# Sliding-window attention and a gated MLP: the first three units in parts of DFF, weight words decoded in place, queues ordered by another pass

## The chip, the cores and the metric

The kernel runs on one core of one Trainium2 chip. The metric is the device time of one execution in microseconds (us); a time that is given for a kernel is the median of several runs. The engines are named as in the profile: PE (TensorE) with its weight loads PEld, DVE (VectorE), ACT (ScalarE), POOL (GpSimd), and SP (SyncE), whose queue issues the transfers between DRAM and the on-chip memory.

## The reference

An attention in which each position sees itself and the 63 positions before it, then a gated MLP with a convolution over three positions:

```python
scores = scale * np.matmul(q, k.transpose(0, 1, 3, 2))   # B=8, H=8, S=576, D=64
mask = (rel >= 0) & (rel < 64)                            # rel = pos_q - pos_k
scores = np.where(mask, scores, -1000000000.0)
scores = scores - np.max(scores, axis=-1, keepdims=True)
attn = np.exp(scores)
attn = attn / (np.sum(attn, axis=-1, keepdims=True) + 1e-09)
x = np.matmul(attn, v)                                    # to [B, S, 512]
h = np.maximum(x @ w_in, 0.0)                             # w_in 512 x 1024
conv_out += conv_w[k] * hp[:, k:k + S, :]                 # k = 0, 1, 2; hp is h with a zero row at both ends of a sequence
gate = 1.0 / (1.0 + np.exp(-conv_out))
out = h * gate @ w_out                                    # w_out 1024 x 512
```

The activations are float32. The three weight tensors are float64, and they come to the chip as words of 64 bits, which the kernel decodes itself.

## The kernel before, in words

**Units.** The 8 x 576 positions are cut into 12 units of 384 (NX). A unit goes through attention, the first matmul with `w_in` (mm1), relu, convolution, sigmoid gate, the second matmul with `w_out` (mm2), and a store. DFF = 1024 is cut into 8 slices of 128 (f, NF), DM = 512 into 4 of 128 (c for mm1's sums, o for mm2's outputs, NC).

**Attention of a unit** has three blocks b of four window tiles. For each block: scores into two PSUM banks (`qk`, L357, called "sc" on PE); the row maximum with the mask on DVE (L364); eight exponentials with their row sums on ACT (L374); a guard on the sums (L377), the reciprocal (L380) and the normalising (L385). Then the weights of the attention are turned over. Units 0 and 1 (`BY_PE = 2`) are "wide": blocks of 128 x 128, turned by six groups of TensorE transposes a unit (L391), each copied out of PSUM by ACT (`untile`, L396). The other units have narrower blocks (96 of 128), which DVE transposes in 32 x 32 squares into `tbuf` (L412), and which 24 small DMAs a unit put into `ub` (`place`, L424). At last values (L488): for each c twelve small matmuls into a bank `acc`, which is split into a larger part `xh` (ACT, L492) and what is left, `xl` (DVE, L495).

**MLP of a unit.** Every large product is made of three: larger by larger, smaller by larger, larger by smaller. So mm1 has for each f 3 x 4 matmuls of 384 columns (L508) into one of the two banks `acc`; relu on ACT (L525, L529) writes `hbuf`; POOL carries the two edge columns from one unit to the next (L514 to L520). For each pair of slices ACT does the middle tap (L535), DVE the side taps (L542), ACT the sigmoid (L549, with a table load where the exponential stood before it) and DVE the gate (L554); ACT and DVE split the result into `gh` and `gl` (L558, L562). mm2 (L571) sums in four banks `po`, 3 matmuls for each f and o, five slices behind mm1 (`LAG`). At the end of a unit ACT and DVE copy the four banks to `ot` (L607, L609) and SP stores it.

**The decoding of weights** (`to_f32`, `weights`): the words of a pair of slices land in one of two staging buffers `bits`, ACT takes the absolute value of the upper half as float (L252), POOL the maximum with a tiny number (L253), DVE shifts (L254) and sets the sign (L256), ACT scales the lower half (L259), DVE adds it (L260). The larger part is cast by ACT (L275) or POOL (L277), the smaller subtracted by DVE (L278). `bits`, `tbuf` and `ot` share one tile, which the profile calls T.

**The order** of every engine's queue is fixed before the run. `queued` goes through all steps as a list scheduler with a cost for each: of the steps that could begin next on an engine it takes the one with the smallest due time `t`. The due times count in slices of mm1; for the first units and the attention they are the numbers of a table, `START`. `SWITCH` and `LEAVE` are its costs for going from one sort of matmul to another and for ACT's tables. At the beginning, where TensorE would wait, it puts in matmuls on a spare tile, whose results nobody reads (`keep_busy`, L216).

Of the kernel before, what the change touches and what calls it, by code (L numbers as in the profile page):

```python
# [28 lines left out]
LAG = 5  # L29
BY_PE = 2  # L30
# [3 lines left out]
TINY = 2.0 ** -15  # L34

LAST = NU - 1
# [10 lines left out]

class Work:


    def __init__(self, t, eng, cost, do, r, w, kind, mb, port):
        self.t, self.eng, self.cost, self.do, self.r, self.w, self.kind, self.mb = t, eng, cost, do, r, w, kind, mb
        self.port = port
        self.needs, self.after, self.ready = 0, [], 0.0
        self.start = self.end_ = 0.0


def queued(works, fill=None):

    import heapq
    writer, readers = {}, {}
    for x in works:
        deps = set()
        for k in x.r:
            if k in writer:  # L70
                deps.add(writer[k])
        for k in x.w:
            deps.update(readers.get(k, ()))
            if k in writer:
                deps.add(writer[k])
        deps.discard(x)
        for d in deps:
            d.after.append(x)
        x.needs = len(deps)
        for k in x.w:  # L80
            writer[k], readers[k] = x, []
        for k in x.r:
            readers.setdefault(k, []).append(x)
    free = {"PE": 0.0, "DVE": 0.0, "ACT": 2.0, "POOL": 0.7, "SP": 1.3}
    state = dict.fromkeys(free)
    waiting = {e: [] for e in free}
    touched = {k: ("", 0.0) for k in [("sc", 0)] + [("acc", i) for i in range(2)] + [("po", i) for i in range(NC)]}
    for x in works:
        if x.needs == 0:
            waiting[x.eng].append(x)  # L90
    dma, port, order, left = 0.0, {"DVE": 0.0, "POOL": 0.0}, [], len(works)
    while left:
        best = None
        for e, ws in waiting.items():
            if not ws:
                continue
            start = max(free[e], min(x.ready for x in ws))
            if best is None or start < best[0]:
                best = (start, e)
        start, e = best  # L100
        x = min((x for x in waiting[e] if x.ready <= start),
                key=lambda x: x.t - (0.5 if x.kind and x.kind == state[e] else 0.0))
        if x.port:
            if e == "POOL" and start < port["DVE"]:
                free[e] = port["DVE"]
                continue
            start = max(start, port["POOL"])
            port[e] = start + x.port
        waiting[e].remove(x)
        if fill and e == "PE" and start < FILL_TO:  # L110
            t = max(free[e], FILL_FROM)
            n = int((start - t) * FILL)

            clean = [(end, k) for k, (by, end) in touched.items() if by != "PE" and end < t]
            if n > 0 and clean:
                order.append(Work(x.t, e, 0.0, fill(n, min(clean)[1]), [], [], None, 0, 0.0))
        turn = SWITCH[e] if e in SWITCH and (x.kind != state[e] if e == "PE" else x.kind and x.kind != state[e]) else 0.0
        if turn and e == "PE" and not x.kind:
            turn = LEAVE
        if e == "PE" or x.kind:  # L120
            state[e] = x.kind
        end = free[e] = start + turn + x.cost * (1.75 if e == "PE" and start < WARM else 1.0)
        if x.mb:
            dma = max(dma, start) + x.mb * 2.7
            end = dma + 1.9
        for k in x.r + x.w:
            if k in touched:
                touched[k] = e, end
        order.append(x)
        left -= 1  # L130
        for y in x.after:
            y.needs -= 1
            y.ready = max(y.ready, end + (0.0 if e == "PE" else 0.06) if y.eng == e else end + 0.2)
            if y.needs == 0:
                waiting[y.eng].append(y)
    return order
# [3 lines left out]
START = {  # L140
    "v0": -34.213,
    "pv0": -15.486,
    "conv": -34.622,
    "bits": ((-44.162, -48.108), (-49.962, -46.523)),
    "qk1": -44.058,
    "v1": -6.318,
    "qk2": 0.918,
    "qk0": (-88.698, -55.197, -55.435),
    "ex0": (-38.484, -35.539, -25.91),
    "sc1": (-35.664, -14.916, -14.661),  # L150
    "ex1": (-10.948, -3.722, -2.234),
    "mask": -13.894,
    "sig": ((5.143, 6.743, 8.637, 10.624), (2.954, 4.077, 7.59, 9.996), (4.046, 6.806, 8.285, 10.314)),
    "in": (-40.063, -38.679, -33.327, -12.569, -5.818),
    "out": (-5.241, -4.847, 7.996, 9.148),
    "pv": ((4.028, 4.396, 3.657, 4.79), (6.11, 6.569, 6.573, 6.956), (3.166, 4.869, 3.456, 4.567)),
    "ex": ((6.203, 9.564, 10.485), (7.867, 9.835, 9.841), (5.299, 6.578, 7.215)),
    "qk": ((1.316, 5.641, 4.209), (5.897, 6.102, 6.617), (3.205, 3.444, 5.13)),
}
SWITCH = {"PE": 0.14, "ACT": 1.28}  # L160
LEAVE = 0.24
PORT_CL = 0.5
WARM = 5.0
FILL, FILL_FROM, FILL_TO = 4.0, 2.0, 110.0
FILL_COLS = 512, 384, 256
# [3 lines left out]
def attention_moe(ctx: ExitStack, tc: tile.TileContext, q, k, v, w_in, conv_w, w_out, out):  # L169
    nc = tc.nc  # L170

# [7 lines left out]
    xh, xl = many(2, [P, NC, NX], F32R, "xh"), many(2, [P, NC, NX], F32R, "xl")  # L179
    hbuf = pool.tile([P, NF, NG + 2], F32, name="hbuf")  # L180
    wih, wil = pool.tile([P, NF, NC, P], F32R, name="wih"), pool.tile([P, NF, NC, P], F32R, name="wil")
    woh, wol = pool.tile([P, NF, DM], F32R, name="woh"), pool.tile([P, NF, DM], F32R, name="wol")
    cw = pool.tile([P, 3, NF], F32, name="cw")
    mask = many(3, [P, P], F32, "mask")
    ident = pool.tile([P, P], F32, name="ident")
    qs = pool.tile([P, NC, NX], F32, name="q")
    ks = pool.tile([P, NC, NX + W], F32, name="k")
# [4 lines left out]
    ghs, gls = many(3, [P, 2, NG], F32R, "gh"), many(3, [P, 2, NG], F32R, "gl")  # L192


    flat = pool.tile([P, 16 * NT * 32 + NC * NG], F32, name="T")
    tbuf = flat[:, :16 * NT * 32].rearrange("p (g j t q) -> p g j t q", g=2, j=4, q=32)
    ot = flat[:, 16 * NT * 32:].rearrange("p (o n) -> p o n", o=NC)
    bits = [flat.bitcast(U32)[:, 4 * DM * i:4 * DM * (i + 1)].rearrange("p (e two) -> p e two", two=2) for i in range(2)]
    T_BITS = (0,), (0, 1)
    w24 = many(2, [P, 2 * DM], F32, "w24")  # L200
    cbits = pool.tile([P, 3 * NF, 2], U32, name="cbits")
    sc = many(2, [P, 512], F32, "sc", psum)
    acc = many(2, [P, 512], F32, "acc", psum)
    po = many(NC, [P, 512], F32, "po", psum)

    spare = pool.tile([P, 512], F32R, name="spare")
    filled = [0]
# [94 lines left out]

    def wide(u):
# [429 lines left out]
```

## Time and profile before

| | |
|---|---|
| time, median of 3 runs | 528.75 us (527.37 to 530.91) |
| the profiled execution, span from its first to its last instruction | 528.6 us |
| TensorE clock granted, mean over the span | 0.994 |
| moved by the DMA queues | 69.94 MB, mean 132 GB/s |
| HBM read and written | 47.73 MB and 9.47 MB |

The profiled execution's own time is its span, 528.6 us; what lies around the span isn't in the profile, and the span is 0.15 us from the median of the runs. The rows in the prediction come from the page of this execution and from questions to its trace. A row of a group (an operation with its line, its count, then busy time and mean ns of one, then the idle time of its engine ahead of it) speaks of the whole span; a row in order of time begins with its start in us and its duration. Line numbers are those of the code above.

### The profile page before, as it was taken

To read this page: it belongs to the slowest core of one execution; us is meant where nothing else is said; L and a number is where in the kernel's file an instruction comes from. 1 tells how busy PE (TensorE), PEld (TensorE's weight loads), DVE (VectorE), ACT (ScalarE), POOL (GpSimd) and SP (SyncE) were. 2 spreads that over 40 slices of the span, in tenths; PEclk is the share of its full clock that TensorE was granted. 3 is DMA by queue.
4 is the path that set the end of the run, shared out by engine and by line. 5 is a ranking of instruction groups with operands and counts; after the bars stand their busy time and mean duration, and the time that the engine had idled before them with its cause. 6 is when DMAs were issued, how large, how long until landed. Compare 5 with 4: busy or idle time off the path is not lost.

```text
span 528.6 us, 14478 instructions
## 1 busy us (share of the span) xinstructions
PE 507.8 (96%) x5646; PEld 486.1 (92%) x5646; DVE 377.7 (71%) x1084; ACT 384.5 (73%) x1017; POOL 105.5 (20%) x192
## 2 busy tenths in 40 slices
PE   6867899999999999999999999999999999999996
PEld 4657799999899999999999999999999999999996
DVE  3998999998668676667767767767767767655552
ACT  1988999788795994696696697687687687544541
POOL 5663645112011120011021021021021021000000
PEclk9998999999999999999999999999999999999999
DMA  8982670265472264172173073083073053010011
GB/s 275 378 276 101 231 258 2 51 203 190 115 269 68 66 206 129 56 275 69 40 288 77 22 256 112 23 287 97 14 279 99 24 165 95 13 61 1 1 61 60
DMA packets 29459, 69.94 MB, mean 132 GB/s; under 512 B 5712, under 2 KB 17616, under 8 KB 29392
## 3 DMA queue, kind: packets, MB, share of 16 engines
q1 hardware_dynamic: 29392, 69.03, 39.6%
q8 instruction: 44, 0.72, 0.6%
q14 instruction: 23, 0.19, 0.1%
HBM read 47.73 MB, written 9.47 MB: 108 GB/s over the span
## 4 chain that ended last, share of the span: by engine, by line
PE 89%; DMA 4%; ACT 3%; DVE 2%; issue 1%; SPq 0%; ACTq 0%
PE po L571 39%; PE acc L508 38%; PE acc L488 6%; PE sc L357 5%; DMA q<-in_q_dram 2%; DMA T<-in_w_in_dram 1%; DVE s L364 1%; ACT ub L396 1%; ACT s L374 0%; ACT w L252 0%; DVE wil L278 0%; DVE w L260 0%; DVE xl L495 0%; DVE s L385 0%; ACT L374 0%
## 5 line engine op out<-in xcount | busy, mean ns | idle before, releaser
L508 PE MATMUL acc<-xh,wih 128*128 128x384 f32 x384 | 132.2, 344 | 1.8 <-ACT hbuf L529 0.9
L542 DVE SCALAR_TENSOR_TENSOR c<-hbuf,cw,c 128x386 f32<-128x386 f32 (+1 forms) x192 | 110.0, 624 | 32.8 <-ACT c L535 32.7
L571 PE MATMUL po<-gh,woh 128*128 128x386 f32 (+1 forms) x384 | 132.3, 345 | 0.0
L508 PE MATMUL acc<-xh,wil 128*128 128x384 f32 x384 | 130.9, 341 | 0.0
L508 PE MATMUL acc<-xl,wih 128*128 128x384 f32 x384 | 130.6, 340 | 0.0
L571 PE MATMUL po<-gh,wol 128*128 128x386 f32 (+1 forms) x384 | 129.8, 338 | 0.0
L571 PE MATMUL po<-gl,woh 128*128 128x386 f32 (+1 forms) x384 | 129.8, 338 | 0.0
L374 ACT ACTIVATE s<-s,nm 128x96 f32<-128x96 f32 (+2 forms) x288 | 105.4, 370 | 5.1 <-DVE nm L364 4.9
L508 PEld LDWEIGHTS acc<-xh,wih 128*128 128x128 f32 x384 | 72.9, 190 | 3.5 <-issue 2.1
L562 DVE TENSOR_TENSOR gl<-c,gh 128x772 fp32r<-128x772 f32 (+1 forms) x48 | 54.9, 1144 | 28.6 <-ACT gh L558 28.3
L571 PEld LDWEIGHTS po<-gh,woh 128*128 128x128 f32 x384 | 72.2, 188 | 2.9
L508 PEld LDWEIGHTS acc<-xl,wih 128*128 128x128 f32 x384 | 73.0, 190 | 0.0
L508 PEld LDWEIGHTS acc<-xh,wil 128*128 128x128 f32 x384 | 72.9, 190 | 0.0
L385 POOL TENSOR_TENSOR s<-s,r 128x768 f32<-128x768 f32 x27 | 39.7, 1471 | 165.4 <-DVE r L380 154.1
L554 DVE TENSOR_TENSOR c<-c,hbuf 128x772 f32<-128x772 f32 (+1 forms) x48 | 47.0, 980 | 36.0 <-ACT c L549 35.9
L571 PEld LDWEIGHTS po<-gl,woh 128*128 128x128 f32 x384 | 72.3, 188 | 0.0
L571 PEld LDWEIGHTS po<-gh,wol 128*128 128x128 f32 x384 | 72.3, 188 | 0.0
L529 ACT ACTIVATE hbuf<-acc 128x384 f32<-128x384 f32 x64 | 30.8, 484 | 46.2 <-PE acc L508 45.9
L549 ACT ACTIVATE c<-c 128x772 f32<-128x772 f32 (+1 forms) x48 | 40.7, 848 | 27.4 <-DVE c L542 27.2
L364 DVE CUSTOM_DVE_ANT_0 s<-sc,mask 128x96 f32<-128x96 f32 (+2 forms) x272 | 51.6, 254 | 9.0 <-POOL mask L328 5.3
L374 ACT ACTIVATION_READ_ACCUMULATOR s<-s,nm 128x1 f32 x288 | 55.2, 192 | 0.0
L535 ACT ACTIVATE c<-hbuf,cw 128x386 f32<-128x386 f32 (+1 forms) x96 | 53.6, 609 | 0.0
(64 smaller groups left out, 576.2 us busy)
## 6 DMA issues: line engine op xcount, KB each, us to landing
v<-in_v_dram SPq DMA_DIRECT2D x24, 768.0 KB, 7.1
ub<-T SPq DMA_DIRECT2D x240, 48.0 KB, 2.0
k<-in_k_dram SPq DMA_DIRECT2D x22, 448.0 KB, 5.6
q<-in_q_dram SPq DMA_DIRECT2D x22, 384.0 KB, 5.8
out_dram<-T SPq DMA_DIRECT2D x8, 772.0 KB, 4.4
T<-in_w_in_dram SPq DMA_DIRECT2D x8, 512.0 KB, 6.9
T<-in_w_out_dram SPq DMA_DIRECT2D x8, 512.0 KB, 5.1
out_dram<-T SPq DMA_DIRECT2D x3, 768.0 KB, 6.2
```

The source lines that it names most:

```text
L364: nc.vector.tensor_tensor_reduce(out=ss[b][:, i, h, o:n], in0=banks_of(u, b)[h][:, i * P + o:i * P + n], in1=mask[m][:, o:n], scale=-0.125 ...
L374: nc.scalar.activation(x, x, AF.Exp, bias=nms[b][:, e], scale=-1.0, accum_out=sms[b][:, e])
L385: on.tensor_tensor(sv, sv, rs[b].unsqueeze(2).broadcast_to([P, 2 * NB, n]), ALU.mult)
L488: nc.tensor.matmul(acc[bank(("v", u, c))][h * D:(h + 1) * D, t * W:(t + 1) * W], vs[:, c, t, h], ub[g][:, 2 * p:2 * p + 2, 2 * t + h], sta ...
L508: nc.tensor.matmul(acc[bank(("m", u, f))][:, :NX], w[:, f, c], x[u % 2][:, c], start=(c == 0 and j == 0), stop=(c == NC - 1 and j == 2))
L529: nc.scalar.activation(hbuf[:, f, o:o + NX], ps[:, :NX], AF.Relu)
L535: nc.scalar.activation(cs[i % 2][:, a, :n], hbuf[:, f, 1:1 + n], AF.Copy, scale=cw[:, 1, f:f + 1])
L542: nc.vector.scalar_tensor_tensor(c, hbuf[:, f, e:e + n], cw[:, e, f:f + 1], c, op0=ALU.mult, op1=ALU.add)
L549: nc.scalar.activation(c, c, AF.Sigmoid)
L554: nc.vector.tensor_tensor(c, c, hbuf[:, 2 * i:2 * i + 2, 1:1 + n], ALU.mult)
L562: nc.vector.tensor_tensor(gls[ring(u, i)][:, :, :n], cs[i % 2][:, :, :n], ghs[ring(u, i)][:, :, :n].bitcast(F32), ALU.subtract)
L571: nc.tensor.matmul(po[o][:, :n], w[:, f, es], x, start=(f == 0 and j == 0), stop=(f == NF - 1 and j == 2))
```

## The change

**The first three units in parts.** `TASKS` replaces "for each unit all eight slices". Units 0, 1 and 2 go over slices 0 and 1 in turn, then over 2 and 3, then over 4 to 7; units 3 to 11 are as before. mm2 sums in PSUM only within a part. The result of a first part is stored plainly by SP (`store`), those of the second and third parts are added to it in DRAM by six transfers that POOL issues (`store_more`). `xh` and `xl` exist three times. All result copies go half to ACT and half to DVE, through one tile `ot`, which now stands by itself.

**Weights.** The words of a slice f are loaded into a tile of their own, `raw_in f` or `raw_out f`, in whose place the larger and the smaller part are put later (`w_in f`, `w_out f`, the same tag). The two buffers in between (`wx`) share tile T with `tbuf` only. POOL's maximum goes; a factor 2^-112 in ACT's absolute value does its work. The list `HI` says which engine casts the larger part of each of nine groups, `DECODE` the groups.

**Attention.** Units 0 to 2 are wide (`BY_PE = 3`) and their queries and keys come block by block from a new input, `first`, packed on the host. Unit 0 is normalised in halves, unit 3 on DVE too (`POOL_FROM = 4`). A `place` DMA is a step of its own.

**Order.** `plan` writes the steps without due times, `link` finds what each waits for, `backward` goes from the end to the beginning and gives each step the latest time at which it may start, `OFF` corrects that for some fifty steps, and `schedule` is the list scheduler with these as priorities, with costs of its own, with a bonus (`STICK`) for a step of the same sort as the last one on PE or ACT, and with a choice of PSUM banks. `START` is left for scores, transposes (`turn`) and values.

```diff
-LAG = 5
-BY_PE = 2
 NB = 4
 NBU = 2 * NT // NB
 MASKED = -8.0e9
-TINY = 2.0 ** -15
...
+BY_PE = 3
+SPLIT = 3
+CUTS = [(0, 2), (2, 4), (4, NF)]
+LAG = 5
+TASKS = [(u, a, b) for a, b in CUTS for u in range(SPLIT)] + [(u, 0, NF) for u in range(SPLIT, NU)]
...
+    def decode(key, fs):
+        n, one = len(fs), len(fs) == 1
+        kx = ("x", turn[0] % 2)
+        buf = turn[0] % 2
+        turn[0] += 1
...
+            load("load_w", (key, f), 0.524, [(key, f), (key, f, "lw")])
+        args = (key, fs, buf)
+        at("ACT", 0.03 + 0.5 * n, 0.14 + 0.5 * n, "magnitude", args, r=raw, w=[kx])
...
+        eng = HI[len(decoded_in)]
...
+    for k, (u, f0, f1) in enumerate(TASKS):
+        if u not in done:
+            done.add(u)
+            attention(u)
...
+        n = width_of(u)
+        x = x_of(u)
+        po = [Group([(4 + o,)]) for o in range(NC)]
+        for f in range(f0, f1):
+            need("in", f)
...
+                for ff in fs:
+                    need("out", ff)
+                    for o in range(NC):
+                        at("PE", 0.527, 0.7, "mm2", (u, ff, o, j, ff == f0, ff == f1 - 1), r=[("gh", g), ("gl", g), ("out", ff, "h"), ("out", ff, "l")] + [("pob", o)],
+                           w=[("po", k, o)], grp=po[o], t=first[k] + ff - f0 + LAG + 0.5 + 0.01 * o)
...
+        part = "more" if f0 else "first"
...
+            at(e, 0.365 if e == "ACT" else 0.477, 0.48 if e == "ACT" else 0.56, "result", (u, o, e), r=[("po", k, o)], w=[("ot", o), ("pob", o)], grp=po[o])
...
+        if part == "more":
+            at("POOL", 1.2, 1.2, "store_more", (u,), r=[("ot", o) for o in range(NC)], w=[("out", u)], mb=1.2)
+        elif u != LAST:
+            load("store", (u,), 0.8, [("out", u)], r=[("ot", o) for o in range(NC)])
...
+def schedule(works, prio, fill=False):
...
+                p = prio[x]
+                if x.kind and x.kind == kind.get(e):
+                    p -= STICK
+                if best is None or s < best[0] - 1e-9:
+                    best = (s, p, x)
+                elif s <= best[0] + 1e-9 and p < best[1]:
+                    best = (best[0], p, x)
...
+def backward(works):
...
+HI = ('POOL', 'POOL', 'POOL', 'POOL', 'ACT', 'ACT', 'ACT', 'DVE', 'POOL')
+DECODE = [('in', (0,)), ('in', (1,)), ('out', (0, 1)), ('in', (2, 3)), ('out', (2, 3)), ('in', (4, 5)),
+          ('out', (4, 5)), ('in', (6, 7)), ('out', (6, 7))]
+HALVED = (0,)
+POOL_FROM = 4
+GUARD_TO = 3
+WARM = 16.0
+FILL, FILL_FROM, FILL_TO = 0.45, 2.0, 110.0
...
+    flat = pool.tile([P, 2 * 3 * 2 * NT * 32], F32, name="T")
+    wx = [flat[:, 2 * DM * i:2 * DM * (i + 1)] for i in range(2)]
+    tbuf = flat.rearrange("p (g j t q) -> p g j t q", g=2, j=3, q=32)
...
+        raws[key, f] = pool.tile([P, DM, 2], U32, name=f"raw_{key}{f}", tag=f"{key}{f}")
...
+    def load_first(u, b):
+        a, n, _ = first_at(b)
+        nc.sync.dma_start(qk[:, a:a + n], first[u, :, a:a + n])
...
+    def to_magnitude(x, hw):
+        nc.scalar.activation(x, hw.bitcast(F32), AF.Abs, scale=2.0 ** -112)
...
+    def to_shift(x):
+        xu = x.bitcast(U32)
+        nc.vector.tensor_scalar(xu, xu, 3, 0x7FFFFFF8, op0=ALU.logical_shift_left, op1=ALU.bitwise_and)
...
+    def larger(kf):
+        wts[kf] = pool.tile([P, 2, DM], F32R, name="w_%s%d" % kf, tag="%s%d" % kf)
+        return wts[kf][:, 0]
...
-        at(t, "POOL", 0.0027 * n + 0.02, lambda: nc.gpsimd.tensor_scalar(x, x, TINY, None, op0=ALU.max), w=kt, port=PORT_CL)
...
-            xu, xu, 3, 0x3FFFFFF8, op0=ALU.logical_shift_left, op1=ALU.bitwise_and), w=kt)
...
+    def store_more(u):
         n = width_of(u)
+        nc.gpsimd.dma_start(out[u, :, :, :n], ot[:, :, :n], accum_op=ALU.add)
...
+    works = plan()
+    late = backward(works)
+    for x in works:
+        late[x] += OFF.get((x.fn,) + x.args[:2], 0.0)
     with tc.manual_schedule():
-        for x in queued(plan, keep_busy):
-            x.do()
+        for x in schedule(works, late, True)[0]:
+            fn[x.fn](*x.args, *([x.grp.banks] if x.grp else []))
```

Three places of the new queues. The first is ACT's queue ahead of the first pairs of gate halves. In both kernels `s`, `sm` are exponentials, `ub` copies of transposes, `hbuf` relu, `c` the middle tap or the sigmoid, `xh` value halves and `gh` gate halves. Before, from the middle of the first two pairs up to the first exponentials of unit 2, which are 96 wide:

```order
L259 ACTIVATE T_100<-T_100 128x1024
L252 ACTIVATE w240_101<-T_100 128x1024
L529 ACTIVATE hbuf_67<-acc0_106 128x384
L529 ACTIVATE hbuf_67<-acc1_107 128x384
L535 ACTIVATE c1_93<-hbuf_67,cw_72 128x386 x2
L396 COPY ub1_62<-po0_108 128x4x4x32
L549 ACT_TABLE_LOAD
L549 ACTIVATE c0_92<-c0_92 128x772
L396 COPY ub1_62<-po1_109 128x4x4x32
L529 ACTIVATE hbuf_67<-acc1_107 128x384
L374 ACT_TABLE_LOAD
L374 ACTIVATE s0_80,sm0_86<-s0_80,nm0_83 128x96 x2
```

After, the same place, up to the first gate half:

```order
L839 ACTIVATE s0_79,sm0_85<-s0_79,nm0_82 128x128 x2
L935 ACTIVATE hbuf_69<-bank0_101 128x384
L945 ACTIVATE c0_91<-hbuf_69,cw_71 128x386 x2
L867 COPY ub1_62<-bank6_107 128x4x4x32
L867 COPY ub0_61<-bank4_105 128x4x4x32
L839 ACTIVATE s0_79,sm0_85<-s0_79,nm0_82 128x128 x2
L727 ACTIVATE raw_out0_653<-raw_out0_653 128x512
L727 ACTIVATE raw_out1_258<-raw_out1_258 128x512
L839 ACTIVATE s2_81,sm2_87<-s2_81,nm2_84 128x128 x8
L957 ACT_TABLE_LOAD
L957 ACTIVATE c0_91<-c0_91 128x772
```

The exponentials of unit 2 now stand around the relu and the middle tap of unit 0's first pair and ahead of its sigmoid; before, those of unit 2 came behind the first sigmoid, with a table load ahead of them. The weight passes work on `raw_out` in its own place instead of T.

The second place is TensorE at a unit in the middle of the program, where the values of one unit stand in the matmuls of another. Before (`ub` is values, `k`, `q` scores of the narrow kind, of which only the first three of 32 are shown; `acc` from `xh` or `xl` is mm1):

```order
L508 MATMUL acc1_107<-xh0_63,wil_69 128x384
L508 MATMUL acc1_107<-xl0_65,wih_68 128x384
L488 MATMUL acc0_106<-ub0_61,v_79 64x64 x12
L488 MATMUL acc1_107<-ub1_62,v_79 64x64 x12
L357 MATMUL sc0_104<-k_78,q_77 32x96
L357 MATMUL sc1_105<-k_78,q_77 32x96
L357 MATMUL sc0_104<-k_78,q_77 32x96
```

After (`gh` and `gl` are mm2):

```order
L978 MATMUL bank6_107<-gl2_98,w_out2_1448 128x386
L978 MATMUL bank7_108<-gh2_95,w_out2_1448 128x386 x2
L978 MATMUL bank7_108<-gl2_98,w_out2_1448 128x386
L893 MATMUL bank0_101<-ub1_62,v_78 64x64 x12
L978 MATMUL bank4_105<-gh2_95,w_out3_1450 128x386 x2
L978 MATMUL bank4_105<-gl2_98,w_out3_1450 128x386
L893 MATMUL bank1_102<-ub0_61,v_78 64x64 x12
```

Two values of a unit with a block of scores right behind them became single values between the matmuls of mm2.

The third place is POOL's queue around the second round of parts, where `hbuf` is the carrying of edge columns and `ot` the result tile:

```order
L925 MEMSET hbuf_69 128x2
L1010 DMA out_0_dram<-ot_99 128x1544
L923 COPY hbuf_69<-hbuf_69 128x2x2
L925 MEMSET hbuf_69 128x2
L1010 DMA out_0_dram<-ot_99 128x1544
L923 COPY hbuf_69<-hbuf_69 128x2x2
L925 MEMSET hbuf_69 128x2
L1010 DMA out_0_dram<-ot_99 512x1x384
L754 CAST w_out6_1709<-T_70 128x512
L754 CAST w_out7_1711<-T_70 128x512
```

Here stand the first three of the six adding transfers. Of before, the beginning of the decoding on the same engine, with the maxima (L253) between guards (L377) and casts (L277):

```order
L253 TENSOR_SCALAR w240_101<-w240_101 128x512
L377 TENSOR_SCALAR sm0_86<-sm0_86 128x8
L253 TENSOR_SCALAR w240_101<-w240_101 128x512
L277 CAST wih_68<-w240_101 128x512
L377 TENSOR_SCALAR sm1_87<-sm1_87 128x8
```

The maxima are gone from POOL's queue, and DMAs that read `ot` have come into it.

## What the change does to the time: the prediction

> **What bounds the kernel now.** I read the page first, then busy time by stage, then TensorE's instructions in order of time, then the chain of waits.
>
> The page: the span and the busy shares.
>
> ```profile
> span 528.6 us, 14478 instructions
> ...
> PE 507.8 (96%) x5646; PEld 486.1 (92%) x5646; DVE 377.7 (71%) x1084; ACT 384.5 (73%) x1017; POOL 105.5 (20%) x192
> ```
>
> TensorE is busy almost throughout, DVE and ACT for three quarters of the span. By stage that differs:
>
> ```profile
> core 0: us, PE busy (x) PEld busy (x) DVE busy (x) ACT busy (x) POOL busy (x), PEclk, DMA share, GB/s
> 0.00:20.00 20.00, 12.86 (x141) 9.39 (x142) 9.92 (x56) 9.00 (x36) 11.90 (x51) 1.00 0.90 321
> 20.00:70.00 50.00, 40.64 (x594) 35.98 (x594) 47.24 (x136) 45.08 (x131) 27.98 (x24) 0.93 0.67 231
> 70.00:110.00 40.00, 40.00 (x372) 39.19 (x372) 38.43 (x89) 35.15 (x77) 13.86 (x16) 1.00 0.25 78
> ```
>
> From 20 to 70 us TensorE has holes while DVE works 47.24 of 50 us; from 70 it has none. TensorE in order of time shows where that turns (L488 is values, L508 the first matmul), and the row behind it counts L508 up to there:
>
> ```profile
> 62.94 0.92 PE L488 MATMUL acc<-ub,v 128*64 128x64 f32 x24 [2.29 <-DVE xl L495]
> ...
> 68.68 0.44 PE L508 MATMUL acc<-xh,wih 128*128 128x384 f32 x1
> ```
>
> ```profile
> 0.00:68.68 68.68, 16.60 (x72) 14.79 (x72) 0.95 0.73 255
> ```
>
> The hole of 2.29 us is the last one; from 68.68 on, with 72 matmuls done, one instruction follows the other. The end, and three steps of a middle unit (L571 is the second matmul, L357 scores), from the chain of waits in order of time:
>
> ```profile
> 301.24 0.93 PE sc L357 x56
> 302.16 2.31 PE acc L508 x12
> ...
> 306.58 1.55 PE acc L488 x48
> ...
> 511.71 12.70 PE po L571 x72
> ```
>
> Seventy-two matmuls take 12.70 us, 0.176 each or 2.11 a dozen; behind scores a dozen takes 2.31: each return from attention to matmuls costs 0.20. A block of scores takes 0.93, two values 1.55. TensorE ends at 511.71 + 12.70 = 524.4, and 4.2 us of copy and store follow. So the time is 68.7 + 455.7 of unbroken TensorE + 4.2 = 528.6: the profiled span, 0.15 under the median of the runs, 528.75. I set time equal to span.
>
> **The change part by part.** I ask the same of the new order: when does TensorE's unbroken run start (M, at the first second matmul, because all before it in the new queue has holes), how much runs behind it (R), and what holes are left.
>
> *R.* Counted in the queues: behind M the new order has 2304 - 48 = 2256 large matmuls, the old behind 68.68 has 2304 - 72 = 2232: +24 x 0.176 = +4.2. One block of scores less (26 for 27; the first of unit 3 is ahead of M): -0.9. Two values less (38 for 40; ten are ahead): -1.55. And returns: the old queue goes back to matmuls 30 times, three for a unit (two values with scores right behind, twice; one scores alone); the new one 45 times, four and six for a unit in turn, since values and scores stand apart. +15 x 0.20 = +3.0. R = 455.7 + 4.2 - 0.9 - 1.55 + 3.0 = 460.4. The last mm1 and the six parts of the second matmul behind it stand as before, so the tail stays 4.2.
>
> *M.* The six transposes that unit 2 now gets on TensorE lie ahead of M, in its holes; so do the 24 small DMAs and four DVE transposes that they replace. What sets M is the ACT queue: ahead of the first gate half (the larger part, L965) it now has the exponentials of three units, some 22 more than before. ACT's own paces, by starts:
>
> ```profile
> 22.64 0.43 ACT L374 ACTIVATE s<-s,nm 128x128 f32<-128x128 f32 x1
> ...
> 26.12 0.40 ACT L374 ACTIVATE s<-s,nm 128x128 f32<-128x128 f32 x1
> ...
> 26.50 1.06 ACT L396 COPY ub<-po 128x512 f32<-128x512 f32 x2
> 27.45 1.20 ACT L252 ACTIVATE w<-T 128x1024 f32<-128x1024 f32 x1
> 28.53 0.86 ACT L492 CAST xh<-acc 128x384 fp32r<-128x384 f32 x2
> 29.26 0.43 ACT L374 ACTIVATE s<-s,nm 128x128 f32<-128x128 f32 x1
> ...
> 47.33 0.84 ACT L529 ACTIVATE hbuf<-acc 128x384 f32<-128x384 f32 x2
> 48.08 1.11 ACT L535 ACTIVATE c<-hbuf,cw 128x386 f32<-128x386 f32 x2
> ...
> 55.76 1.28 ACT L549 ACT_TABLE_LOAD   x1
> 57.06 0.85 ACT L549 ACTIVATE c<-c 128x772 f32<-128x772 f32 x1
> ...
> 62.56 0.85 ACT L558 CAST gh<-c 128x772 fp32r<-128x772 f32 x1
> ```
>
> From 22.64 to 26.12 are nine steps: 0.387 an exponential. In the new queue up to that gate half: 72 exponentials 27.8; 18 copies of transposes at 0.475 (two from 26.50 to 27.45), 8.55; eight passes over weights of 512 at half of 1.08, 4.3; eight value halves at 0.365, 2.9; two relu at 0.375 and the middle tap 1.0, 1.8; conv weights about 0.25; table, sigmoid and gate half 1.28 + 0.85 + 0.85. Sum 48.6 us; then DVE's smaller gate half and hand-offs, about 1.1.
>
> ACT's idle time is the unknown. Up to 70 us the old one idles (20 - 9.00) + (50 - 45.08) = 15.9 us, and that gives M = 48.6 + 15.9 + 1.1 = 65.6 as the upper bound. Two of its waits are for weights behind other loads or for a staging buffer:
>
> ```profile
> 13.05 0.68 ACT L252 ACTIVATE w<-T 128x512 f32<-128x512 f32 x1 [5.37 <-DMA T<-in_w_in_dram]
> ...
> 40.98 1.16 ACT L252 ACTIVATE w<-T 128x1024 f32<-128x1024 f32 x1 [2.66 <-DMA T<-in_w_in_dram]
> ```
>
> The new SP queue issues the first weight part second instead of ninth, and every part has its own place. Without the first wait M is 60.2, without both 57.6; I take the middle, 58.9. The lower bound: ACT starts at about 6, when the first weights can land, and never waits: 6 + 48.6 + 1.1 = 55.7.
>
> *Holes behind M.* Between M and the last weights (out 6, 7) DVE is the second bound, and the new order gives it no slack. Its costs from the old rows (page means, then DVE in order of time):
>
> ```profile
> L542 DVE SCALAR_TENSOR_TENSOR c<-hbuf,cw,c 128x386 f32<-128x386 f32 (+1 forms) x192 | 110.0, 624 | 32.8 <-ACT c L535 32.7
> L562 DVE TENSOR_TENSOR gl<-c,gh 128x772 fp32r<-128x772 f32 (+1 forms) x48 | 54.9, 1144 | 28.6 <-ACT gh L558 28.3
> L554 DVE TENSOR_TENSOR c<-c,hbuf 128x772 f32<-128x772 f32 (+1 forms) x48 | 47.0, 980 | 36.0 <-ACT c L549 35.9
> ```
>
> ```profile
> 81.98 0.72 DVE L254 TENSOR_SCALAR w<-w 128x1024 uint32<-128x1024 uint32 x1
> 82.73 1.23 DVE L256 SCALAR_TENSOR_TENSOR w<-T,w 128x1024 uint32<-128x1024 uint32 x1
> 83.87 2.21 DVE L542 SCALAR_TENSOR_TENSOR c<-hbuf,cw,c 128x386 f32<-128x386 f32 x4
> ...
> 94.48 0.92 DVE L554 TENSOR_TENSOR c<-c,hbuf 128x772 f32<-128x772 f32 x1
> ...
> 97.07 0.92 DVE L562 TENSOR_TENSOR gl<-c,gh 128x772 fp32r<-128x772 f32 x1
> ```
>
> In that stretch stand six weight pairs (a shift of 0.75 and three passes of 1.14, by starts: 25), eight conv pairs at 2.2 (17.5), eight gates and seven smaller halves at 0.92 (13.8), and twelve result copies, five half row maxima, three normalisings and four value halves, some 0.6 each, 14.5: 70.8 us. With the page means, which hold waits inside instructions (conv pair 2.5, gate 0.98, half 1.14), it is 75.2. TensorE's own work there is 384 large matmuls, 67.6, two scores, two values and three or four returns: 71.7 us. DVE also idles for its partners: by the stages above 2.76 + 1.57 us in the 90 from 20 to 110, so 3.4 here. The holes are then 0 if it never idles, 70.8 + 3.4 - 71.7 = 2.5 by paces and 75.2 + 3.4 - 71.7 = 6.9 by means. I take 2.5, because the POOL maximum over the weights leaves:
>
> ```profile
> L253 POOL TENSOR_SCALAR w<-w 128x1024 f32<-128x1024 f32 x7 | 24.8, 3540 | 12.3 <-ACT w L252 12.3
> ```
>
> That pass becomes a factor in ACT's first pass, at no cost there, and 3.54 us leave the latency of every pair. Its 24.8 us lay beside DVE's conv and weight work, where I look for the difference of means and paces; if that is elsewhere, 6.9 it is.
>
> *Stores.* Units 0 to 2 now store three times each: 24 result copies more, half on ACT, half on DVE (counted above), and six adding DMAs from POOL, which nothing in this trace shows. The nearest rows, and the one queue there is beside code loading:
>
> ```profile
> ub<-T SPq DMA_DIRECT2D x240, 48.0 KB, 2.0
> out_dram<-T SPq DMA_DIRECT2D x8, 772.0 KB, 4.4
> ...
> q1 hardware_dynamic: 29392, 69.03, 39.6%
> ```
>
> A result tile may be overwritten only when its store has landed. The tightest place is the second round: from unit 0's results to unit 1's DVE has 6.6 us of other work queued, from unit 1's to unit 2's 6.2. With the plain 4.4 us the store is hidden and costs nothing; beyond about 6.4 each us costs one in both gaps. Behind the waiting copy stand DVE's weight passes, and TensorE waits for the bank. No reason excludes a quicker one, which would gain nothing. [...]
>
> *Unit 3.* Its transposes share a tile with the decoding and so stand behind the last pair; twelve small DMAs (2.0 us each to landing) lie between them and the first values, with some 10 us of matmuls beside them. Hidden, if SP issues one in 0.65 us; a slower SP belongs to the upper end of the holes.
>
> *Sum.* 58.9 + 460.4 + 4.2 + 2.5 = 526.0: the unbroken run starts ten us earlier, but 4.7 us more work stands in it and 2.5 of holes come back.
>
> **The rivals.** Within 1% (523.4 to 534.0) is no change here; less could not be told from run to run (527.37 to 530.91).
>
> Forecast, 526 (523.5 to 530.5 with M or the holes at their ends), chance 0.54.
>
> The early queues run without waits: M at 55.7 and no holes: 55.7 + 460.4 + 4.2 = 520.3; anything with M plus holes under 58.8 is faster by over 1%. For it: the two load waits are 8.0 of ACT's 15.9 idle us. Against it: DVE and ACT feed each other in these blocks, and a fixed order turns each late part into a wait. Chance 0.27.
>
> The adding store holds the results: it counts from a landing of about 10.4 us, where 526 + 2 x (10.4 - 6.4) passes 534; with 12 us it is 526 + 11.2 = 537. For it: result copies in front of DVE's weight work, one tile. Against it: the plain store needs 4.4. Chance 0.12.
>
> The early part gains nothing: M at its upper bound, 65.6, with 2.5 to 7 of holes: 532.7 to 537.2. For it: some 22 exponentials more ahead of M. Against it: the two load waits. Chance 0.07.
>
> **How the numbers follow.** Faster 0.27; same 0.54; slower 0.12 + 0.07 = 0.19. The range 519 to 536 leaves out a part of the two slower cases and little below. The likeliest time is 526.
>
> **What would show it.** In the new profile: L978 (second matmul) starts first at 56 to 61 us; its chain is ACT and DVE before that and TensorE behind; 29 fillers stay ahead. A pair of middle units takes 0.8 us more than in the old one (four returns). L253's pass is gone and POOL idles early. Waits of L978 for DVE between 60 and 135 us add up to 2 to 3 us. Result copies that wait for a store would show as DVE and ACT waiting on a DMA into out_dram between 105 and 130 us. I am wrong if M lies outside 55 to 62, if the holes are over 7 us, or if the middle units are no slower than before.

## The result, and the profile after

The changed kernel takes 543.6 us (median of 4 runs, 541.4 to 545.7), beside 528.5 for the kernel before: the ratio is 1.027 (95% interval 1.023 to 1.032). Forecast were 526.0 and no change. The profiled execution is the slowest of the four, 545.7; the four were granted 0.987 to 0.994 of the clock, the slower the less.

The page of the kernel after, in parts: span, busy shares, granted TensorE clock in 40 slices.

```profile
span 544.0 us, 14309 instructions
...
PE 514.4 (95%) x5573; PEld 485.0 (89%) x5573; DVE 376.5 (69%) x1128; ACT 382.0 (70%) x1039; POOL 88.8 (16%) x191
...
PEclk9999999999999989998999997999999999999999
```

TensorE is as busy as before by its share, but in the middle slices, not at the beginning, the clock now falls. TensorE in order of time, the start of the second matmul and three places in the middle (L893 is values; in brackets the hole ahead of it, that is TensorE's idle time, and what ended it):

```profile
58.85 0.62 PE L978 MATMUL bank<-gh,w_out 128*128 128x386 f32 x2
...
189.59 2.49 PE L893 MATMUL bank<-ub,v 128*64 128x64 f32 x48 [2.36 <-DMA ub<-T]
...
244.73 2.83 PE L893 MATMUL bank<-ub,v 128*64 128x64 f32 x48 [2.93 <-issue]
...
331.07 2.83 PE L893 MATMUL bank<-ub,v 128*64 128x64 f32 x48 [3.71 <-DMA ub<-T]
```

So M, the start of the second matmul, is where the forecast put it. The loss lies behind. By stages (columns as in the prediction's stages), then from M to the end:

```profile
58.85:110.00 51.15, 50.84 (x386) 49.30 (x383) 50.11 (x100) 46.09 (x96) 9.93 (x18) 1.00 0.37 127
110.00:150.00 40.00, 37.04 (x299) 34.30 (x299) 35.02 (x72) 27.86 (x66) 7.11 (x14) 1.00 0.59 116
150.00:200.00 50.00, 47.64 (x551) 45.42 (x550) 31.23 (x96) 33.81 (x89) 8.18 (x13) 0.97 0.60 153
200.00:250.00 50.00, 47.07 (x569) 45.01 (x568) 31.19 (x104) 30.13 (x83) 7.35 (x13) 0.97 0.37 111
...
300.00:350.00 50.00, 46.29 (x560) 44.10 (x559) 32.13 (x112) 33.73 (x96) 9.59 (x13) 0.93 0.41 122
```

```profile
58.85:544.00 485.15, 466.73 (x4836) 446.39 (x4832) 329.15 (x913) 329.61 (x847) 72.14 (x124) 0.99 0.39 113
```

Of the 485.15 us TensorE works 466.73; 18.4 are idle: 4.2 behind the last matmul and 14.2 of holes. From 150 to 500 us DVE and ACT are at 60 to 75%, so neither is the bound there. What TensorE waited for behind M (total, times, longest):

```profile
PE bank L893 <- DMA ub<-T: 7.3, 3, 3.7
PE bank L893 <- issue: 2.9, 1, 2.9
PE bank L978 <- ACT ot L986: 2.0, 2, 1.6
PE bank L978 <- DVE ot L986: 0.6, 1, 0.6
```

Most of this is values that wait for the small DMAs (`place`) of their unit. For the hole of 2.93 us the profile names no releaser ("issue"), but the last small DMA of that unit landed at 244.64 us, just ahead of the values at 244.73. SP's queue ahead of the hole at 244.7, in order of time (L886 the small DMAs, L693 a query load, L1005 a store, L701 a load of v):

```profile
222.02 14.46 SPq L886 DMA_DIRECT2D ub<-T  x23
236.53 0.59 SPq L693 DMA_DIRECT2D qk<-in_q_dram  x1
237.22 0.36 SPq L1005 DMA_DIRECT2D out_dram<-ot  x1
237.63 3.28 SPq L886 DMA_DIRECT2D ub<-T  x1
241.01 6.91 SPq L701 DMA_DIRECT2D v<-in_v_dram  x2
```

Twenty-three of the unit's 24 small DMAs are issued in a row; the last one stands behind 384 KB of queries and a store of 772 KB. It is 48 KB. Of the same place in unit 7, from the chain of waits, then the page's row of all small DMAs (the median from issue to landing is its last column):

```profile
324.31 6.62 DMA ub<-T
```

```profile
ub<-T SPq DMA_DIRECT2D x216, 48.0 KB, 1.9
```

It took 6.6 us to land instead of 1.9, and the one at 237.63 took 7.0. Behind the holes of units 4, 5 and 7 the clock is halved for 3.4 us, or twice that, 13.7 us in all; at unit 4 (the granted clock is the column after the engines):

```profile
187.00:190.00 3.00, 0.64 (x16) 0.44 (x16) 1.71 (x2) 0.58 (x1) 0.07 (x2) 1.00 0.81 194
190.00:193.40 3.40, 3.40 (x46) 3.28 (x42) 1.11 (x2) 0.96 (x2) 0.00 (x0) 0.50 0.28 61
193.40:198.00 4.60, 4.60 (x66) 4.34 (x65) 0.88 (x2) 1.87 (x4) 0.00 (x0) 1.00 0.42 151
```

### The profile page after: what moved, and what is told of

It is laid out like the page before. It is cut to its first block, busy times and chain, and to the rows that moved or that the text cites. A ratio compares the mean times of both kernels' runs of the same rounds, so it can differ in the third digit from the quotient of the medians.

```text
span 544.0 us, 14309 instructions
## 1 busy us (share of the span) xinstructions
PE 514.4 (95%) x5573; PEld 485.0 (89%) x5573; DVE 376.5 (69%) x1128; ACT 382.0 (70%) x1039; POOL 88.8 (16%) x191
## 4 chain that ended last, share of the span: by engine, by line
PE 68%; DVE 12%; ACT 8%; DMA 5%; issue 3%; SPq 1%; POOL 1%; POOLq 0%; ACTq 0%
PE bank L978 30%; PE bank L910 28%; PE bank L893 6%; PE bank L816 5%; DMA ub<-T 3%; DVE c L953 3%; ACT s L839 3%; DMA out_dram<-ot 3%; DVE s L828 1%; DVE s L856 1%; SPq L886 1%; DVE c L961 1%; ACT T L716 1%; DVE T L731 1%; DVE gl L970 1%
## 5 line engine op out<-in xcount | busy, mean ns | idle before, releaser
L978 PE MATMUL bank<-gh,w_out 128*128 128x386 f32 (+1 forms) x768 | 202.6, 345 | 3.0 <-ACT ot L986 2.0
L910 PE MATMUL bank<-xh,w_in 128*128 128x384 f32 x768 | 198.1, 339 | 1.2 <-DVE r L850 0.8
L978 PEld LDWEIGHTS bank<-gh,w_out 128*128 128x128 f32 x768 | 138.0, 189 | 8.6 <-ACT ot L986 3.4
L910 PEld LDWEIGHTS bank<-xh,w_in 128*128 128x128 f32 x768 | 138.2, 188 | 4.8 <-issue 2.1
L978 PE MATMUL bank<-gl,w_out 128*128 128x386 f32 (+1 forms) x384 | 130.1, 339 | 0.0
L910 PE MATMUL bank<-xl,w_in 128*128 128x384 f32 x384 | 129.1, 336 | 0.0
L978 PEld LDWEIGHTS bank<-gl,w_out 128*128 128x128 f32 x384 | 72.7, 189 | 0.0
L910 PEld LDWEIGHTS bank<-xl,w_in 128*128 128x128 f32 x384 | 72.1, 188 | 0.0
L828 DVE CUSTOM_DVE_ANT_0 s<-bank,mask 128x96 f32<-128x96 f32 (+2 forms) x288 | 56.1, 259 | 18.4 <-PE bank L816 12.7
L893 PEld LDWEIGHTS bank<-ub,v 128*64 128x64 f32 x1152 | 39.4, 147 | 18.0 <-issue 15.5
L893 PE MATMUL bank<-ub,v 128*64 128x64 f32 x1152 | 43.3, 235 | 11.2 <-DMA ub<-T 7.3
```

What stands on the lines that cost most here:

```text
L828: nc.vector.tensor_tensor_reduce(out=ss[b][:, i, h, o:n], in0=banks[bank[h]][:, i * P + o:i * P + n], in1=mask[m][:, o:n], scale=-0.125, s ...
L893: nc.tensor.matmul(banks[bank[0]][h * D:(h + 1) * D, t * W:(t + 1) * W], vs[:, c, t, h], ub[g][:, 2 * p:2 * p + 2, 2 * t + h], start=True, ...
L910: nc.tensor.matmul(banks[bank[0]][:, :NX], w[:, a, c], y[x][:, c], start=(c == 0 and j == 0), stop=(c == NC - 1 and j == 2))
L978: nc.tensor.matmul(banks[bank[0]][:, :n], wts["out", f][:, w, es], x, start=(start and i == 0), stop=(stop and i == 2))
```

## The experiments

Except for the last run, all edits are to the changed kernel; of each only the lines that matter are shown. The kernel before, run on the same chips, took 527.8 to 528.1 in these calls.

**The last small DMA first.** A pass over the planned order moves that last `place` ahead of the query load and the store:

```diff
-        for x in schedule(works, late, True)[0]:
+        for x in last_place_first(schedule(works, late, True)[0]):
```

> Edit: in units 5, 7, 9 and 11 the last of the 24 small DMAs that put the attention weights into ub is issued ahead of the load of queries and the store that stood before it on SP. Theory A (the time behind the start of the second matmul goes in holes of values that wait for these DMAs, and in half clock behind the holes): the holes of 2.9 us at 244.7 and 3.7 us at 331.1 go, most of the 1.2 us of unit 9, and with them three of the four windows of 3.4 us at clock 0.5, which cost 1.7 us each; 543.6 - 7.8 - 5.1 = about 530.7. Theory B (the 24 DMAs are late as a whole, since SP issues one in 0.6 to 0.77 us; what stands ahead of the last one does not decide): the waits stay within 1 us of what they are, 541 to 544. Theory C (the adding stores made the kernel slower): no change, 543 to 544.

Measured: 533.0. The holes of units 5, 7 and 9 are gone; what is left of this wait is unit 4's 2.2 and 0.3 in unit 8, with one half-clock stretch behind the first:

```profile
PE bank L893 <- DMA ub<-T: 2.6, 2, 2.2
```

One DMA in four units, out of its place in a queue, cost 10.6 us, holes and half clock together. Theory A holds, within 2.3 us; B falls, and C as the only cause.

**Fillers in the holes.**

```diff
+        if x.fn == "values" and x.args in IN_HOLE:   # {(4, 0): 11, (5, 0): 14, (7, 0): 18, (9, 0): 6}
+            yield Work("PE", 0.0, 0.0, "fill", (IN_HOLE[x.args], x.grp.banks[0]))
```

> Edit: spare matmuls of 512 columns stand directly ahead of the values that waited for small DMAs (11 in unit 4, 14 in unit 5, 18 in unit 7, 6 in unit 9; 0.22 us each, so about as long as the holes); nothing else moves. Values cannot start earlier by it. Theory A: the granted clock is halved by the idle time itself, so the four windows of 3.4 us at 0.5 go and 4 x 1.7 = 6.8 us with them: about 537. Rival: the slow matmuls behind the holes have another cause (operands, traffic of DMAs): the clock windows stay, and the time is 543.6 or up to 1 us more by fillers that run over.

Measured: 543.7. The same stretch as above, in this kernel:

```profile
190.00:193.40 3.40, 3.40 (x43) 2.67 (x44) 1.47 (x2) 0.33 (x1) 0.00 (x0) 1.00 0.64 163
```

The clock is 1.00 there and in the stretches behind the holes of units 5 and 7, where it was 0.50 to 0.51 without the fillers, so it is the idle time that halves it: that part of A holds. (Its clock is 0.997 over the span and 1.00 from M on, so what was lost of it lies ahead of M, long before these places.) The time did not fall. In the profiled execution the way from M to the end is 3.2 us shorter, not 6.8 (481.99 for 485.15): the fillers take 11.9 us for 10.2 of holes, and holes of 1.1 and 1.35 us come up elsewhere; M is 1.6 later.

```profile
60.43:542.42 481.99, 471.91 (x4885) 449.70 (x4881) 328.93 (x913) 329.27 (x847) 74.46 (x124) 1.00 0.39 114
```

By its time alone the run could not tell A from the rival; the granted clock does.

**Plain stores of the later parts.**

```diff
-        nc.gpsimd.dma_start(out[u, :, :, :n], ot[:, :, :n], accum_op=ALU.add)
+        nc.gpsimd.dma_start(out[u, :, :, :n], ot[:, :, :n])
```

> Edit: the six stores of later parts write plainly instead of adding, from the same place in POOL's queue; this leaves the sums over the parts of units 0 to 2 out. Theory A: the result copies that waited for such a store cost TensorE 2.0 + 0.6 us in the profile, so at most 2.6 us plus what a shorter wait lets move up: 540.5 to 543.6. Theory C (the adding transfer holds the results and with them DVE and ACT): landing falls from 7.2 to about 4 us and the time by 8 us or more, under 536.

Measured: 537.4, between the two; the interval of the ratio to the kernel before, 1.014 to 1.023, leaves open whether that is 2% slower. DMA issues of the kernel after, then of this one (KB each, median us from issue to landing):

```profile
out_dram<-ot POOLq DMA_DIRECT2D x4, 772.0 KB, 7.2
```

```profile
out_dram<-ot POOLq DMA_DIRECT2D x4, 772.0 KB, 4.1
```

Of the waits for result copies the hole of 1.56 us goes; those of 0.44 and 0.57 stay (0.41, 0.59), so they were not the store's. Unit 4's hole shrinks from 2.36 to 0.20. The trace of the kernel after shows a likely reason: one adding store is on its way from 181.13 to 188.95 us, and SP's small DMAs for unit 4 that are issued from 182.0 to 187.0 take long to land, the first line, beside those issued ahead of it, the second:

```profile
DMA to landing us min/median/max: 2.7/4.5/5.8
DMA to landing us min/median/max: 1.9/1.9/3.2
```

The one of them that landed at 189.58 is the last ahead of the values at 189.59. The plain store in this place lands in 5.1 instead of 7.8 us. The holes of units 5 and 7 stay (2.82, 3.44), but there is half clock behind the second alone. So the adding stores have a share: in the two profiled executions holes behind M fall by 4.2 us (14.2 to 10.0) and TensorE's working time by 5.7 (466.73 to 461.04). C as the main cause falls, since the last-DMA edit alone, which leaves the stores as they are, brought 10.6.

**Each adding store in two halves.**

```diff
+        for o in (slice(0, 2), slice(2, NC)): nc.gpsimd.dma_start(out[u, :, o, :n], ot[:, o, :n], accum_op=ALU.add)
```

> Edit: each of the six adding stores is issued as two transfers, results 0 and 1 and results 2 and 3. With plain stores in their place the kernel took 537.4 (landing 4.1 instead of 7.2 us). If the first copies of the next unit are what waits, the first half lands in 4 to 5 us and most of those 6.2 us come back: 538 to 540. If the copies of results 2 and 3 wait as long as before, right behind the others, under 2 us come back: 541.6 to 543.6, less about nothing for twelve issues on a POOL that idles.

Measured: 540.2, near the lower of the two: about half of the 6.2 us came back. The copies wait 1.04 instead of 1.56 us in the second round, and unit 4's hole falls to 0.55.

**No small DMAs from unit 4 on.**

```diff
...
+        placed += x.fn == "place"
+        if x.fn != "place" or placed <= 24:
+            yield x
```

> Edit: from unit 4 on the small DMAs that put the turned attention weights into ub are left out (192 of 216; the values of these units then use the weights of unit 3). Theory A: values no longer wait; 10.7 us of holes and four windows of half clock (6.8 us) go: 543.6 - 17.5 = about 526, the forecast. If another thing holds the middle units as well (result copies, the clock without holes, more returns to the large matmuls), it stays above 532.

Measured: 528.9; the profiled execution took 530.6, with a span of 528.5, of which M is 61.12; its clock is 0.997 over the span and 1.00 behind M. From M to the end:

```profile
61.12:528.46 467.34, 460.23 (x4836) 440.60 (x4832) 328.12 (x913) 329.16 (x847) 73.26 (x124) 1.00 0.32 97
```

TensorE works 460.23 us behind M, with the same instructions as in the changed kernel: the forecast's R is 460.4. The other 6.5 of 466.73 fit the 13.7 us of half clock there. The expected 526 left out the 2 us by which these times stand above their spans.

**All three repairs.** The last DMA first, unit 4's DMAs for the first half of the heads first, stores in halves.

```diff
+        for x in first_half_first(last_place_first(schedule(works, late, True)[0])):
```

> Edit: the last small DMA of a unit ahead of the query load and the store (as in the run that measured 533.0), unit 4's small DMAs for the first half of the heads ahead of those for the second, and the adding stores in halves. Theory A (what is left behind the start of the second matmul is holes and half clock): of 533.0 the hole of 2.2 us of unit 4 goes with its window of half clock (1.7), and up to 2 of the 2.6 us behind result copies: 527 to 529.5, level with the kernel before (527.96 on that chip). Rival (the chain of unit 4 from scores to values is too long as a whole): its hole moves to its second pair of values, and the time stays at 531 or more.

Measured: 529.2, ratio to the kernel before 1.002 (1.000 to 1.005). Unit 4's hole is gone. In the profiled execution, of 532.2, a new one stands one unit earlier:

```profile
159.53 1.36 PE L893 MATMUL bank<-ub,v 128*64 128x64 f32 x24 [2.96 <-DMA ub<-T]
```

**Unit 3 as well**, and then **two queues in all units**: the transposes of unit 3 directly behind the result copy (a pass that isn't shown), and six of 24 small DMAs from POOL, first in unit 3, then in all.

```diff
+        (nc.gpsimd if soft(g, i) else nc.sync).dma_start(ub[g][o:o + HW, i], tbuf[HW * i:HW * (i + 1), g, j])
```

> Edit: the mended kernel of 529.2, and in unit 3 the last two DVE transposes directly behind the result copy ahead of them (about 1.7 us earlier) and six of the twelve small DMAs that follow issued by POOL beside SP (SP took 9.1 us for twelve, so some 3 us earlier). In the mended kernel's trace unit 3's second pair of values waits 2.96 us for these at 159.5, with a window of half clock behind it (1.7). Theory A (waits for small DMAs are what is left): both go, 529.2 - 3.0 - 1.7 = about 524.5, below the 528.06 of the kernel before; in executions of the mended kernel in which the clock was not halved only the 3.0 are to be had: 526. Rival (DVE's result copies and gate halves, now behind the transposes, hold TensorE instead, or POOL's transfers land later than SP's): 529 or more.

> Edit: in all units from 3 on six of the 24 small DMAs are issued by POOL beside SP (in the run of 528.93 only in unit 3). In that run's trace TensorE was 4.28 us ahead of the mended kernel's after unit 4, and 2.66 at the end: the waits came back in small pieces in units 6, 8 and 10. If they are waits for SP's bursts, the lead stays and the time falls by 1.6 to about 527.3. If POOL's issues stand in the way of its normalising or of the edge columns, which are later in its queue, the time goes up, over 530.

Measured: 528.9 and 528.8 (ratios 1.001 and 1.001, intervals 1.000 to 1.003 and 0.999 to 1.003). The hole of unit 3 went, with its half clock; the medians did not follow as forecast. The forecast of 524.5 took what it saw in an execution of 532.2 from a median of 529.2; between the profiled executions the time fell from 532.2 to 529.5. In the first of the two the lead of 4.28 us behind unit 4 was given back in pieces of 0.2 to 0.5 us in units 6 to 10. In the second they are gone by its trace, and TensorE works as long behind M as with no such DMAs at all:

```profile
59.09:526.76 467.67, 460.49 (x4836) 440.62 (x4832) 329.13 (x913) 329.10 (x847) 104.07 (x184) 1.00 0.41 118
```

In the second 3.4 us of holes are left behind M, 2.7 of them ahead of 150 us. So 528 to 529 is what this order gives with little left to wait for. Why the medians of the two are equal, when their profiled spans are 527.7 and 526.8, stays open; that is within what single executions differ by (527.6 to 531.1 in the second).

**Units whole.** `CUTS = [(0, NF)]`, planned anew, last DMA first.

> Edit: units 0 to 2 go over all eight slices at once, as the others do, so there are no adding stores; the planner orders that, and the last small DMA of a unit stands ahead of the store, as in the run of 533.0. Theory (the parts bring an earlier unbroken run, and cost 24 result copies and the adding stores): the run starts about where the kernel before has it, at 68.7, and 68.7 + 455.7 + 3.0 for the returns + 4.2 + some 3 to 6 of holes and half clock = 535 to 538 for the span, 537 to 540 for the time. Rival (the parts cost more than they bring): under 532.

Measured: 539.9, 6.9 above the same kernel in parts (533.0). TensorE in order of time:

```profile
52.78 1.94 PE L861 MATMUL bank<-ident,s 128*128 128x128 f32 x8 [3.08 <-DVE s L856]
...
62.87 0.41 PE L910 MATMUL bank<-xh,w_in 128*128 128x384 f32 x1 [1.87 <-POOL w_in L754]
64.75 0.44 PE L910 MATMUL bank<-xh,w_in 128*128 128x384 f32 x1 [1.48 <-DVE w_in L751]
...
72.28 0.62 PE L978 MATMUL bank<-gh,w_out 128*128 128x386 f32 x2
```

The first matmuls wait for their weights again, and the second matmul starts 13 us later. So the parts do what they are for. But this kernel is also 11.8 above the kernel before, which has whole units as well: the other changes lose more than the 6.9 that the parts win. Which of them does was not tried.

**More work for ACT.** Its first pass over the words of out 0 and 1 three times.

> Edit: ACT does its first pass over the words of out 0 and 1 three times instead of once, four instructions of about 0.54 us more, 2.2 us, ahead of the first sigmoid. If ACT's queue sets the start of the second matmul, as the prediction has it, that start goes from 58.9 to about 61 and the time from 543.6 to about 545.7. If DVE or the transposes set it, the start moves by less than 1 us and the time by nothing that can be measured.

Measured: 546.3, 2.7 more; the second matmul starts 2.4 later. In the eight traces with the same early queues and no early half clock M lies between 58.85 and 59.52 (the two others, 60.43 and 61.12, have a clock of 0.997 over the span and 1.00 behind M), so the shift is clear of that spread: ACT's queue sets M.

```profile
61.25 0.63 PE L978 MATMUL bank<-gh,w_out 128*128 128x386 f32 x2
```

**Values apart**, on the kernel without small DMAs.

> Edit: on the kernel without the small DMAs from unit 4 on (528.94, clock not halved in most runs) the second values of eight pairs stands behind one more step of the second matmul, so that TensorE goes back from attention to large matmuls 57 instead of 49 times; nothing else moves. By the prediction's price of 0.20 a return: 8 x 0.20 = 1.6 more, 530.5. If a return costs nothing beyond what the pair costs anyway: 528.9.

Measured: 531.4, 2.4 more; behind M TensorE works 462.99 for 460.23, 2.76 or 0.35 a separation.

```profile
59.11:529.48 470.37, 462.99 (x4836) 440.85 (x4832) 328.40 (x913) 330.06 (x847) 72.14 (x124) 1.00 0.32 97
```

Unit 4's pair in the kernel without this edit, then with it:

```profile
189.25 1.62 PE L893 MATMUL bank<-ub,v 128*64 128x64 f32 x48
190.80 0.62 PE L978 MATMUL bank<-gh,w_out 128*128 128x386 f32 x2
```

```profile
187.19 0.92 PE L893 MATMUL bank<-ub,v 128*64 128x64 f32 x24
188.04 0.62 PE L978 MATMUL bank<-gh,w_out 128*128 128x386 f32 x2
188.50 0.34 PE L978 MATMUL bank<-gl,w_out 128*128 128x386 f32 x1
188.77 0.92 PE L893 MATMUL bank<-ub,v 128*64 128x64 f32 x24
```

A pair takes 1.55 from start to start, a single value 0.85: the second way into values costs 0.15, and with the prediction's 0.20 for the return that makes the 0.35.

**The kernel before, a second time.**

> The kernel before, unchanged, for a second trace. The forecast went from its profiled span, 528.6, in which the unbroken run starts at 68.68 behind two windows of half clock (47.5 and 64.5); its times in the other calls are 1.75 above the span, and their median of 528 belongs to spans near 526.2. If the windows differ from execution to execution, this trace shows the run starting near 66.5 with the same 455.7 behind it; if the span itself was misjudged elsewhere, the start stays at 68.7 and what lies behind it is shorter.

Measured: 528.05. Its unbroken run starts at 65.92, 2.8 earlier than in the first trace, and the work behind is the same, 455.67 and 455.64:

```profile
65.92 0.44 PE L508 MATMUL acc<-xh,wih 128*128 128x384 f32 x1
```

```profile
65.92:525.84 459.92, 455.67 (x4924) 442.14 (x4920) 321.82 (x898) 332.13 (x857) 65.90 (x120) 1.00 0.36 114
```

## Why the prediction was wrong, point by point

- *M = 58.9, set by ACT.* Right: 58.85, and 2.2 us more of ACT made it 2.4 later. The exact number is partly luck: the middle between 57.6 and 60.2 was a choice, and two sizes cancelled. Up to the end of the first gate half, at 56.86, ACT works 50.4 us and not 48.6, and idles 6.5 and not 9.2; the matmul follows 2.0 behind it and not 1.1.
- *R = 460.4.* Right as a sum: 460.23 where nothing disturbs it. The price of its 15 returns is not settled. A pair of values set apart costs 0.35 in the run above, not 0.20. But where nothing disturbs it, a pair of middle units, with four returns more than before, takes 81.1 and 80.9 us (values at 272.98, 354.09 and 435.00 in the run without small DMAs) for 80.5 in the kernel before (296.39 to 376.92): 0.4 to 0.6 more, where 0.8 was forecast.
- *Tail 4.2.* Right: the last matmul ends at 539.8 of 544.0.
- *Holes 2.5.* This step failed. The prediction looked for holes between M and the last weights, and the size is about what came, 3.1 (0.30 + 0.44 + 1.56 + 0.21 + 0.57), by luck: half of it is the wait for an adding store, which the prediction priced apart, and not DVE's surplus of work. Behind that it had none, by silence: from 70 us on the old trace has none, and the new order was held to be as dense. The waits of the small DMAs came into one paragraph, for unit 3, and only into the upper end of the range. They were 10.2 us in units 4 to 9 (2.36 + 2.93 + 3.71 + 1.24; another 0.5 went to a value half of ACT), and the clock, for which the prediction had no term, took 6.5 more in this execution. The forecast plus these: 526.0 + (14.2 - 2.5) + 6.5 = 544.2, for a span of 544.0. SP's new queue, with a store between the 23rd and the 24th small DMA, could be read before the run for units 5, 7 and 9 (unit 4's wait is another, told under the adding store); R was counted on TensorE's queue alone.
- *The adding store.* The landing was 6.9 and 7.0 us in the second round, above the 6.4 from which the prediction counts: 0.5 + 0.6 = 1.1 by its rule. The trace has a single hole of 1.56, behind the first of them. The medians to landing are 7.2 for the adding store and 4.1 for the plain one, a factor of 1.76. In the time the stores cost 6.2, more than their own hole. What the prediction had no price for is an adding store that is on its way beside the small DMAs of unit 4; this is the likeliest part of the rest, with the half clock behind unit 4's hole, but it was not tried apart. The rival, landings of 10.4 us or more in the second round, did not come.
- *Time equal to span.* In the runs here the time is 1.7 to 2.2 above the span, and the shown execution of before began its run 2.8 later than the second trace. A typical span of before is 526, so the 2.6 us that the forecast gained were not there: with nearly every wait removed, the change is level with the kernel before.

## What to carry to other kernels

Where an order is planned anew, read the queue of the engine that issues DMAs as closely as the engine that is the bound: one small transfer behind a store decides when a whole unit may start (here it took 6.6 and 7.0 us to land in two units instead of 1.9, and moving it in four was worth 10.6). TensorE's work, its start and its tail, summed from old rows, came within 1 us here, with terms that cancelled; the holes in between came from the longest chain of each unit (scores, softmax, transposes, transfers), which has to be laid beside the time that TensorE gives it. A long store that is on its way at the same time belongs to that chain, even from another queue: beside one from POOL the small DMAs on SP took a median of 4.5 us to land instead of 1.9. Moving TensorE ahead takes that time from the chain, so a repair at one unit shows the next wait, and only part of it reaches the end (of a lead of 4.28 us behind unit 4, 2.66).

## What was not expected of the hardware

In the trace of the changed kernel the holes of 2.36 and 2.93 us have a stretch of 3.4 us at clock 0.50 behind them, and the one of 3.71 has 6.8 us. In the first trace of the kernel before, the hole of 2.29 us at 62.94 has 3.4 us of it, from 64.5 on. In three more executions the matmuls behind a hole show it by taking longer: 24 values 1.55 us instead of 0.92 behind 2.54 us (the kernel before, a second time), 1.36 instead of 0.92 behind 2.96 (all three repairs), and eight transposes 1.94 instead of 1.07 behind 3.08 (units whole). With plain stores, 2.82 us have no such stretch behind them. Single holes under 2 us behind the first 60 us of the changed kernel have none (1.24 us at 416 and 1.56 at 121), but two close together can have one: 1.95 and 0.93 us ahead of 48 us in the kernel before, with clock 0.50 from 47.5 to 50.9, and 1.87 and 1.48 us in the run with whole units, where two large matmuls then took 0.84 us instead of 0.51. So no bound comes out of these traces. Filling the holes with spare matmuls removed the stretches (1.00 instead of 0.50 to 0.51). That an adding transfer from POOL lands 3.1 us behind a plain one of its size (medians of 7.2 and 4.1), and that its issue takes POOL 0.85 to 1.22 us instead of 0.53 to 0.78 in the run with plain stores, was new as well.
